# Second exchange of batch 0 through DRAM, products from PSUM, and S1 chunks between the visits

## The chip, the cores and the metric

One core of one Trainium2 chip runs the whole kernel. The metric is the time of one execution on the device, in microseconds (us); the median over runs counts. Engines are named as in the profile: PE is TensorE (PEld its weight loads), DVE VectorE, ACT ScalarE, POOL GpSimd, SP SyncE.

## What is computed

The first half filters each of 8 batches along its 3072 positions in the frequency domain; the second half is a maxout network of two branches over all 24,576 rows.

```python
X = np.fft.rfft(x, axis=1)                       # x: (8, 3072, 256), float32
F = (filt_r + 1j * filt_i)[None, :, :]           # 1537 frequencies x 256 channels
y = np.fft.irfft(X * F, n=x.shape[1], axis=1)
h1, h2 = y.reshape(B * S, D) @ w1, y.reshape(B * S, D) @ w2   # w1, w2: (256, 1024)
out = np.maximum(h1, h2) @ w_out                 # w_out: (1024, 256)
```

## The kernel before, in words

**The transform.** 3072 = 128 x 24, so each transform is done in four steps of matrix products. Step 1 (`f1`) multiplies x by the 128-point table C1 for six chunks of four of the 24 columns; a chunk is called an S1 chunk. The result `at` is written to DRAM (`ad`) and read back in another order as `bt` (`f1_read`): the first exchange. Step 2 (`s2`) applies the 24-point tables U for eight sets of frequencies; a set takes two PSUM banks, `px`. VectorE multiplies px by the filter F into `pq` (`mul`, made of `half` calls). Step 3 (`s3`) multiplies pq by VT into four PSUM banks `pz`, for two sets at a time; these go as `zt` to DRAM (`zd`) and come back as `zr` (`z_read`): the second exchange. s2, mul and s3 for two sets are called a visit; a batch has four. Step 4 (`s4`) multiplies zr by G1 and gives `yt`, 512 rows of y.

**The network.** max(h1, h2) = h2 + relu(h1 - h2). So the kernel keeps Wd = w1 - w2, Wo = w_out and M = w2 @ w_out. `moe_h` computes a block `ph` = Wd^T y and its relu `gt`; `moe_o` sums gt @ Wo and y @ M in `po` and copies it to `ot`, which GpSimd's queue writes out. Column j of block j is taken from Wd with a step of eight columns (L501), since rows p x 8 + c of Wo lie together.

**Order.** All engines run their instructions in the order in which the program emits them. After a prologue for batch 0 comes a loop of 49 tiles of 8 steps; each step has one moe_h, one moe_o of the tile before, and whatever `plan` has put there by hand: s4 at the steps of `z4`, the f1 chunks at `first`, the visits at `visits` or at 48b - 45 + 8v, with the second set's products two steps later and s3 five or six steps later. Which of ScalarE and VectorE copies at, gt and ot is chosen by `pick`, a planner that adds up booked durations; yt and zt are fixed, half each. In the loop, four PSUM banks (`pp`) serve f1, s2, s3 and s4, two serve ph and two po. SyncE issues ad, bt, zd and zr; GpSimd issues x loads, Wo and the output.

**Batch 0** differs. Its step 1 (`f1_0`) writes transposed results into AT, which TensorE transposes into bt (`t1`), so the first exchange stays on the chip. Sets 1, 3, 6 and 7 are copied from PSUM to SBUF by ScalarE (`xs0`), and their products are made from there (`from_xs`): five by GpSimd, three by VectorE; the other sets' products are made from PSUM. Step 3 (`s3_0`) has 128 matmuls of 48 columns a visit and writes the transposed ZT, copied mostly by ScalarE, and `t2` transposes ZT into zr: 8 transposes before the loop, 40 within its steps 0, 2 and 4. Chunk 0 of batch 1 runs before the loop. GpSimd loads batch 1's six x chunks and Wo after its products, and then makes both halves of Wd; x chunks for batch 2 follow as buffers come free.

## Time and profile before

| what | value |
|---|---|
| median of 3 runs | 551.79 us (549.17 to 553.81) |
| the profiled execution | 554.73 us |
| its span, first to last instruction | 553.0 us |
| mean granted TensorE clock | 0.969 |
| first ph of the loop | 63.49 us |
| ph's weight loads | 768, median 144 ns |

The profile shows one execution. A group line gives the line in kernel.py, the engine, the operation, what is written and read, the shape, the count, the busy time, the mean duration in ns, and the idle time of the engine just before with what ended it; a busy TensorE is not one at its peak, since matmuls overlap. Timeline lines give start and length in us, and in brackets the idle time before and its releaser. "issue" is time in which the profile shows nothing that the engine waited for. The clock is the share of the full TensorE clock that was granted.

### The profile page before, as it was taken

Reading aid. Unit: us, or ns where it says so; the run is one execution under the profiler, and the core shown is the slowest. Engines: PE = TensorE matmul, PEld = TensorE weight load, DVE = VectorE, ACT = ScalarE, POOL = GpSimd, SP = SyncE. Lnnn points to the kernel's source line nnn. Section 1 sums busy time; section 2 is a strip of 40 time slices with the busy share of each in tenths; the row PEclk is TensorE's granted clock in tenths of the full one; section 3 lists DMA queues with packets and bytes.
Section 4 is the critical chain, followed back from the end, with each engine's and each line's share of the span. In section 5 each row is a group of like instructions: output and inputs, shape, how many; then the busy total and the mean of one; then the engine's idle time right before and its main releaser. Section 6 shows DMA issues by size and latency. Waiting matters only on the chain.

```text
span 553.0 us, 15465 instructions
## 1 busy us (share of the span) xinstructions
PE 504.2 (91%) x6693; PEld 374.4 (68%) x6693; DVE 329.6 (60%) x541; ACT 348.9 (63%) x609; POOL 76.8 (14%) x127
## 2 busy tenths in 40 slices
PE   3634799998999999998999999999999999999995
PEld 2523567775677767776777777777777777777774
DVE  8397458772587557863867378665776386622220
ACT  8634656575465756675666666676667566666662
POOL 6296001100110011000110011101100000000000
PEclk9975799999899999999999999999999999999998
DMA  7969376768776698579786897769877854421111
GB/s 153 150 193 186 86 146 133 194 174 215 132 163 168 210 210 178 144 227 158 180 185 168 216 186 170 179 213 175 181 172 218 161 148 135 124 106 40 77 77 76
DMA packets 68382, 88.56 MB, mean 160 GB/s; under 512 B 4489, under 2 KB 48674, under 8 KB 67274
## 3 DMA queue, kind: packets, MB, share of 16 engines
q1 hardware_dynamic: 54138, 49.03, 38.2%
q0 software_dynamic: 14176, 38.54, 28.6%
q8 instruction: 52, 0.85, 0.6%
q14 instruction: 16, 0.13, 0.1%
HBM read 53.48 MB, written 47.19 MB: 182 GB/s over the span
## 4 chain that ended last, share of the span: by engine, by line
PE 83%; DMA 9%; issue 2%; ACT 2%; DVE 2%; POOL 1%; SPq 0%; DVEq 0%; POOLq 0%; ACTq 0%
PE ph L501 30%; PE po L524 28%; PE po L519 7%; DMA bt<-ad 6%; PE pz L367 5%; PE py L487 3%; PE pa L310 3%; PE px L331 3%; DMA xb<-in_x_dram 2%; DMA ad<-at 1%; PE pt L410 1%; DVE pq L344 1%; PE pz L456 1%; PE pt L472 1%; POOL xb L109 0%
## 5 line engine op out<-in xcount | busy, mean ns | idle before, releaser
L507 ACT ACTIVATE gt<-ph 128x512 bf16<-128x512 f32 x320 | 191.1, 597 | 117.8 <-PE ph L501 113.1
L501 PE MATMUL ph<-yt,Wd 128*128 128x512 bf16 x768 | 232.7, 385 | 0.6 <-ACT yt L97 0.5
L524 PE MATMUL po<-Wo,gt 128*128 128x256 bf16 x1536 | 230.5, 273 | 0.0
L524 PEld LDWEIGHTS <-gt 128*128 128x128 bf16 x1536 | 150.7, 98 | 49.4 <-issue 0.5
L501 PEld LDWEIGHTS <-Wd 128*128 128x128 bf16 x768 | 94.2, 146 | 23.1 <-issue 12.2
L344 DVE TENSOR_TENSOR pq<-px,Fr 120x512 bf16<-120x512 f32 x120 | 81.2, 680 | 13.1 <-PE px L331 12.1
L535 POOL DMA_DIRECT2D out_dram<-ot x47 | 25.2, 537 | 437.5 <-ACT ot L97 392.5
L344 DVE TENSOR_TENSOR pq<-px,Fi 120x512 bf16<-120x512 f32 x120 | 80.6, 677 | 0.0
L505 DVE TENSOR_SCALAR gt<-ph 128x512 bf16<-128x512 f32 x64 | 43.9, 686 | 53.0 <-PE ph L501 34.8
L519 PE MATMUL po<-M,yt 128*128 128x256 bf16 x384 | 73.5, 273 | 0.0
L99 DVE CAST zt<-pz 112x512 bf16<-112x512 f32 x56 | 36.1, 686 | 52.8 <-PE pz L367 30.5
L101 DVE TENSOR_SCALAR yt<-py 128x512 bf16<-128x512 f32 x48 | 33.2, 691 | 51.4 <-PE py L487 51.4
L519 PEld LDWEIGHTS <-yt 128*128 128x128 bf16 x384 | 37.7, 98 | 36.2 <-issue 0.5
L97 ACT ACTIVATE ot<-po 128x512 f32<-128x512 f32 x81 | 48.4, 598 | 12.9 <-ACT yt L97 7.4
L97 ACT ACTIVATE zt<-pz 112x512 bf16<-112x512 f32 x56 | 30.4, 594 | 27.1 <-PE pz L367 27.1
L99 DVE CAST at<-pa 128x512 bf16<-128x512 f32 x42 | 28.9, 688 | 14.4 <-PE pa L310 14.3
L97 ACT ACTIVATE yt<-py 128x512 bf16<-128x512 f32 x48 | 29.0, 603 | 4.2 <-PE py L487 4.1
L331 PE MATMUL px<-bt,U 48*32 48x256 bf16 x1024 | 22.7, 276 | 9.3 <-DMA bt<-ad 7.4
L367 PE MATMUL pz<-pq,VT 24*64 24x256 bf16 x1792 | 30.4, 271 | 0.0
L97 ACT ACTIVATE at<-pa 128x512 bf16<-128x512 f32 x42 | 25.1, 597 | 8.1 <-PE pa L310 8.0
L487 PE MATMUL py<-G,zr 128*128 128x128 bf16 x384 | 29.4, 219 | 0.2 <-DMA ad<-at 0.2
L109 POOL DMA_DIRECT2D xb<-in_x_dram x48 | 26.2, 556 | 12.6 <-PE py L487 12.6
(111 smaller groups left out, 264.7 us busy)
## 6 DMA issues: line engine op xcount, KB each, us to landing
out_dram<-ot POOLq DMA_DIRECT2D x47, 512.0 KB, 4.1
xb<-in_x_dram POOLq DMA_DIRECT2D x48, 256.0 KB, 6.2
ad<-at SPq DMA_DIRECT2D x42, 256.0 KB
bt<-ad SPq DMA_DIRECT2D x28, 384.0 KB
zd<-zt SPq DMA_DIRECT2D x56, 192.0 KB
zr<-zd SPq DMA_DIRECT2D x28, 384.0 KB
w2f<-in_moe_w_dram SPq DMA_DIRECT2D x1, 1024.0 KB
w1f<-in_moe_w_dram SPq DMA_DIRECT2D x1, 1024.0 KB
```

The costliest lines, as they stand in the source:

```text
L97: S.activation(dst, src, AF.Copy, scale=1.0 if scale is None else scale)
L99: V.tensor_copy(dst, src)
L101: V.tensor_scalar(dst, src, scale, None, OP.mult)
L331: TE.matmul(px[dr][32 * q:32 * q + 32, D * ri:D * ri + D], U[64 * dr:64 * dr + 48, s, ri, q], bt[b][64 * dr:64 * dr + 48, 4 * s + q], star ...
L344: V.tensor_tensor(pq[i][0:120, dr].rearrange("p (r d) -> p r d", r=2), px[dr][0:120].rearrange("p (r d) -> p r d", r=2), F[i][0:120, dr, s ...
L367: TE.matmul(pz[q][64 * dr:64 * dr + 64, D * si:D * si + D], VT[32 * q:32 * q + 24, s, o, 64 * dr:64 * dr + 64], pq[i][32 * q:32 * q + 24, ...
L487: TE.matmul(py[dc][:, 128 * n:128 * n + 128], zr[b][:, 4 * i + n, 128 * dc:128 * dc + 128], G1, start=True, stop=True)
L501: TE.matmul(ph, Wd[:, dc, j::8], y_[:, dc].rearrange("p a b -> p (a b)"), start=(dc == 0), stop=(dc == 1))
L505: V.tensor_scalar(gt[tt][:, j], ph, 0.0, None, OP.max)
L507: S.activation(gt[tt][:, j], ph, AF.Relu)
L519: TE.matmul(p_, y_[:, dc, n], M[:, dc], start=(dc == 0), stop=False)
L524: TE.matmul(p_, g_[:, jj, 128 * n:128 * n + 128], Wo[:, jj], start=False, stop=(jj == 7))
```

## The change

- Batch 0's second exchange goes through DRAM as the other batches' does: s3 takes the place of s3_0, with a choice of copying engines for each visit, z_read is emitted one visit later, and t2, ZT and the plan's t2 steps are gone.
- Set 7 is no longer copied to SBUF: its s2 moves behind the other sets' products, and VectorE makes its products from PSUM, like all of its products now. GpSimd makes the other product of set 6, between the first three and the last three loads of batch 1's x.
- `warm(n)` emits n matmuls of 512 columns into a PSUM bank that nobody reads: 14 during step 1, 3 after each s3 of batch 0, 6 ahead of the loop.
- Wd's columns are stored in block order when it is computed, so that moe_h reads 128 contiguous columns; GpSimd computes one half of Wd, VectorE the other, after batch 0's s3. w2's bf16 copy moves behind them.
- AT moves into the pool of bt, its memset ahead of f1_0; the pq of sets 1 and 3 lie in the setup pool.
- In the loop, batch 1's six chunks run at steps 0 to 5. Batch 2's are put between the visits of batch 1, and those of batch b at 48b - 88, -80, -72, -64, -62 and -61: four of them between the visits of batch b - 1, a step before its s3. f1_read follows two and three steps after. The tables of hand-set steps shrink: batches 2 and 3 get the regular visits, tiles 7 to 17 the regular s4 steps. x loads of batches 3 to 7 are planned five steps earlier. batch 1's last z_read comes a step later.

```diff
--- before.py
+++ after.py
@@ -273,9 +273,9 @@
     def load_wo():
         G.dma_start(out=Wo, in_=moe_w_out.rearrange("(p c) j -> p c j", c=8))
 
-    def prep_wd():
-        for dc in range(2):
-            G.tensor_tensor(Wd[:, dc], w1f[:, dc], w2f[:, dc], OP.subtract)
+    def prep_wd(E, dc):
+        E.tensor_tensor(Wd[:, dc].rearrange("p (c h) -> p c h", c=8), w1f[:, dc].rearrange("p (h c) -> p c h", c=8),
+                        w2f[:, dc].rearrange("p (h c) -> p c h", c=8), OP.subtract)
 
     def prep_w2b():
         for dc in range(2):
@@ -356,7 +356,7 @@
             for i in range(2):
                 half(b, s, i, (dr,))
 
-    def s3(b, v, force=None):
+    def s3(b, v, engines=("act", "dve")):
         pz = banks("pz", 4)
         for si in range(2):
             s = 2 * v + si
@@ -372,7 +372,7 @@
             zd[b] = dram.tile([T, 2, 48, D], BF16, tag="zd", name="zd")
         zt = zpool.tile([128, 2, 4, D], BF16, tag="zt", name="zt")
         for q in range(4):
-            e = ("act", "dve")[q % 2]
+            e = engines[q % len(engines)]
             copy(zt[0:112, :, q], pz[q][0:112].rearrange("p (s d) -> p s d", s=2), 512, force=e)
             book(e, 640)
         for dr in range(2):
@@ -386,9 +386,7 @@
         SP.dma_start(out=zr[b][32 * v:32 * v + 32], in_=src[32 * v:32 * v + 32])
 
 
-    AT = init.tile([128, 2, 2, 64, T], BF16, tag="AT", name="AT")
-    ZT = bpool.tile([128, T, D], BF16, tag="bt", name="ZT")
-    ZV = ZT.rearrange("p t d -> p (t d)")[:, 0:6144].rearrange("p (c t m) -> p c t m", c=2, t=T)
+    AT = bpool.tile([128, 2, 2, 64, T], BF16, tag="bt", name="AT")
 
     def f1_0(c, engines):
         pa = banks("pa")
@@ -418,62 +416,31 @@
         if pool is apool:
             pq_[0, s] = [pool.tile([128, 4, D], BF16, tag="at", name="pq").rearrange("p a d -> p (a d)")
                          .rearrange("p (a c) -> p a c", a=2) for _ in range(2)]
+            return
+        if pool is init:
+            pq = init.tile([128, 2, 2, 512], BF16, tag="pq%d" % s, name="pq")
         else:
-            pq = pool.tile([128, 2, 2, 512], BF16, tag="zt" if pool is zpool else "pq", name="pq")
-            pq_[0, s] = [pq[:, i] for i in range(2)]
+            pq = pool.tile([128, 2, 2, 512], BF16, tag="pq", name="pq")
+        pq_[0, s] = [pq[:, i] for i in range(2)]
 
     xs_ = {}
 
-    def xs0(s, slot, k=0):
-        if slot == "AT":
-            if s == 6:
-                xs_[slot] = init.tile([128, 2, 2, 512], FP32, tag="AT", name="xs")
-            xs_[s] = xs_[slot][:, k]
-        else:
+    def xs0(s, slot):
+        if slot:
             xs = init.tile([128, T, 2, J, 2], FP32, tag=slot, name="xs")
             xs_[s] = xs.rearrange("p t o j h -> p (t o j h)")[:, 0:1024].rearrange("p (a c) -> p a c", a=2)
+        else:
+            xs_[s] = init.tile([128, 2, 512], FP32, tag="xs", name="xs")
         for dr in range(2):
             S.activation(xs_[s][0:120, dr], px_[0, s][dr][0:120], AF.Copy)
 
+    def warm(n):
+        pd, = banks("pd", 1)
+        for i in range(n):
+            TE.matmul(pd, C1, xb[0, 0][:, 0:2].rearrange("p a b -> p (a b)"), start=True, stop=True)
+
     def from_xs(E, s, i):
         product(E, pq_[0, s], xs_[s], i, s)
-
-    pz_ = {}
-
-    def pz0(v):
-        pz_[v] = banks("pz", 4)
-
-    def s3_0(v, engines):
-        pz = pz_[v]
-        for si in range(2):
-            s = 2 * v + si
-            pq = pq_.pop((0, s))
-            for dc in range(2):
-                for dr in range(2):
-                    for n, (o, i, ri) in enumerate(((0, 0, 0), (2, 1, 1), (1, 0, 1), (1, 1, 0))):
-                        for q in range(4):
-                            c = ((dc * 2 + si) * 2 + dr) * 48
-                            TE.matmul(pz[q][:, c:c + 48],
-                                      pq[i][32 * q:32 * q + 24, dr, D * ri + 128 * dc:D * ri + 128 * dc + 128],
-                                      VT[32 * q:32 * q + 24, s, o, 64 * dr:64 * dr + 48], start=(n == 0), stop=(n == 3))
-        for q in range(4):
-            copy(ZV[:, :, 8 * v + q:8 * v + q + 5:4], pz[q][:, 0:384].rearrange("p (c s m) -> p c s m", c=2, s=2), 384,
-                 force=engines[q % len(engines)])
-
-    def t2(n0, n1):
-        if n0 == 0:
-            zr[0] = zrpool.tile([128, N2, D], BF16, tag="zr", name="zr")
-        w = 2 if n0 == 0 else 4
-        for h, n in enumerate(range(n0, n1, w)):
-            pt = bank16("pt")[:, 0:w]
-            for i in range(w):
-                for dc in range(2):
-                    zc = ZV[:, dc].rearrange("p t m -> p (t m)")
-                    TE.transpose(pt[:, i, 128 * dc:128 * dc + 128], zc[:, n + i:n + i + 127 * N2 + 1:N2], I128)
-            if h % 2 == 0:
-                V.tensor_copy(zr[0][:, n:n + w], pt)
-            else:
-                S.activation(zr[0][:, n:n + w], pt, AF.Copy)
 
 
     yt, gt, po, ot = {}, {}, {}, {}
@@ -498,7 +465,7 @@
         y_ = yt[tt]
         ph = psh.tile([128, 512], FP32, tag="ph", name="ph")
         for dc in range(2):
-            TE.matmul(ph, Wd[:, dc, j::8],
+            TE.matmul(ph, Wd[:, dc, 128 * j:128 * j + 128],
                       y_[:, dc].rearrange("p a b -> p (a b)"), start=(dc == 0), stop=(dc == 1))
         pe(430)
         if pick(594, 684) == "dve":
@@ -552,11 +519,13 @@
         load_x(0, c)
     table_c()
     table_u()
+    V.memset(AT[:, :, :, 48:].rearrange("p c a m t -> p (c a) (m t)"), 0.0)
     for c in range(6):
         f1_0(c, ("act", "dve") if c > 4 else ("act", "act"))
         if c < 2:
             fill_f(S, 1, 2048 + 1024 * c, 3072 + 1024 * c)
-    V.memset(AT[:, :, :, 48:].rearrange("p c a m t -> p (c a) (m t)"), 0.0)
+        else:
+            warm(3 if c < 5 else 2)
     load_f(G, 1, (2, 0))
     load_f(SP, 1, (1, 3))
     load_w(SP)
@@ -572,7 +541,7 @@
     t1(2)
     t1(3)
     for s in (1, 3):
-        pq0(s, zpool)
+        pq0(s, init)
     for s in (0, 2, 4, 5):
         pq0(s, pqpool)
     for s in (6, 7):
@@ -582,9 +551,7 @@
     fix_f()
     half(0, 0, 0)
     s2(0, 6)
-    xs0(6, "AT")
-    s2(0, 7)
-    xs0(7, "AT", 1)
+    xs0(6, None)
     table_v()
     s2(0, 4, 5)
     from_xs(G, 1, 0)
@@ -592,27 +559,31 @@
     from_xs(G, 6, 0)
     from_xs(G, 1, 1)
     from_xs(G, 3, 1)
-    for c in range(6):
+    for c in range(3):
         load_x(1, c)
+    from_xs(G, 6, 1)
+    for c in range(3, 6):
+        load_x(1, c)
+    prep_wd(G, 0)
     load_wo()
-    prep_wd()
     half(0, 4, 0)
     half(0, 5, 0)
-    from_xs(V, 7, 0)
     V.memset(F[1][0:1, 0, 0], 0.0)
-    half(0, 0, 1)
-    half(0, 2, 1)
-    half(0, 4, 1)
-    half(0, 5, 1)
-    from_xs(V, 6, 1)
-    from_xs(V, 7, 1)
+    for s in (0, 2, 4, 5):
+        half(0, s, 1)
+    s2(0, 7)
+    half(0, 7, 0)
+    half(0, 7, 1)
     for v in range(4):
-        if v == 2:
-            prep_w2b()
-        pz0(v)
-        s3_0(v, ("act",) if v < 3 else ("act", "dve"))
+        s3(0, v, (("act",), ("act",), ("dve",), ("act", "dve"))[v])
+        if v:
+            z_read(0, v - 1)
+        warm(3)
+    z_read(0, 3)
+    prep_wd(V, 1)
+    prep_w2b()
     prep_w2t()
-    t2(0, 4)
+    warm(6)
     setup.close()
     pp = ctx.enter_context(tc.tile_pool(name="pp", bufs=4, space=bass.MemoryType.PSUM))
     psh = ctx.enter_context(tc.tile_pool(name="psh", bufs=2, space=bass.MemoryType.PSUM))
@@ -620,8 +591,6 @@
     ypool = ctx.enter_context(tc.tile_pool(name="ypool", bufs=4))
     gpool = ctx.enter_context(tc.tile_pool(name="gpool", bufs=2))
     opool = ctx.enter_context(tc.tile_pool(name="opool", bufs=2))
-    for c in range(1):
-        f1(1, c, force=("act", "dve"))
     s4(0)
 
 
@@ -634,24 +603,18 @@
         for c in range(6):
             plan(0, 48 * b + step + every * c, load_x, b, c)
 
-    plan(0, 0, t2, 4, 8)
-    plan(0, 2, t2, 8, 16)
-    plan(0, 4, t2, 16, 24)
     plan(0, 6, prep_m)
-    z4 = {1: 3, 2: 8, 3: 11, 4: 18, 5: 25, 6: 46, 7: 52, 8: 61, 9: 69, 10: 77, 11: 85, 12: 93}
-    z4.update({tt: 8 * tt - 7 for tt in range(13, 18)})
+    z4 = {1: 3, 2: 8, 3: 11, 4: 18, 5: 25, 6: 46}
     for tt in range(1, 6 * B):
         plan(0, z4.get(tt, 8 * tt - (5 if tt % 6 == 0 else 6)), s4, tt)
-    first = {1: (0, 1, 2, 3, 4), 2: (39, 40, 41, 42, 43, 44), 3: (86, 87, 88, 89, 90, 91), 4: range(131, 137)}
-    visits = {1: (12, 19, 26, 33), 2: (54, 62, 70, 78), 3: (100, 108, 116, 124)}
+    first = {1: range(6), 2: (16, 23, 30, 37, 39, 40)}
+    visits = {1: (12, 19, 26, 33)}
     for b in range(1, B):
         if b > 1:
-            plan_x(b, -94, 5)
-        ns = first.get(b, range(48 * b - 62, 48 * b - 56))
-        for c, n in zip(range(6 - len(ns), 6), ns):
+            plan_x(b, -94 if b == 2 else -99, 5)
+        n = 48 * b
+        for c, n in enumerate(first.get(b, (n - 88, n - 80, n - 72, n - 64, n - 62, n - 61))):
             plan(0, n, f1, b, c)
-        plan(0, n + 2, f1_read, b, 0)
-        plan(0, n + 3, f1_read, b, 1)
         for v in range(4):
             n = visits[b][v] if b in visits else 48 * b - 45 + 8 * v
             plan(0, n, s2, b, 2 * v, 2 * v + 1)
@@ -661,7 +624,11 @@
             if v:
                 plan(0, n, z_read, b, v - 1)
             plan(0, n, s3, b, v)
-        plan(0, n + (4 if b > 1 else 3), z_read, b, 3)
+        plan(0, n + 4, z_read, b, 3)
+    for b in range(1, B):
+        n = {1: 5, 2: 40}.get(b, 48 * b - 61)
+        plan(0, n + 2, f1_read, b, 0)
+        plan(0, n + 3, f1_read, b, 1)
 
     clock.update(pe=0.0, act=0.0, dve=0.0)
     for tt in range(6 * B + 1):
```

## The prediction, made before the changed kernel was run

> **What bounds the kernel now.** I read the page first (engine shares, slices, chain), then the busy time by stage, then TensorE's timeline at the places where a stage has holes, then the waits, SyncE's timeline, and Wd's tile.
>
> The page:
> ```profile
> PE 504.2 (91%) x6693; PEld 374.4 (68%) x6693; DVE 329.6 (60%) x541; ACT 348.9 (63%) x609; POOL 76.8 (14%) x127
> PE   3634799998999999998999999999999999999995
> PEclk9975799999899999999999999999999999999998
> PE 83%; DMA 9%; issue 2%; ACT 2%; DVE 2%; POOL 1%; SPq 0%; DVEq 0%; POOLq 0%; ACTq 0%
> ...
> L524 PEld LDWEIGHTS <-gt 128*128 128x128 bf16 x1536 | 150.7, 98 | 49.4 <-issue 0.5
> ```
> TensorE is the bound from the fifth slice on; the other engines have a third of their time free. So there are three places to win: the first 63 us, where TensorE is mostly idle; the few holes later (the 9% DMA); and the spacing of the products themselves.
>
> Busy time by stage (PE, PEld, DVE, ACT, POOL, granted clock, DMA share, GB/s):
> ```profile
> 40.00:44.00 4.00, 2.33 (x158) 1.89 (x161) 4.00 (x8) 1.19 (x4) 4.00 (x8) 0.50 0.44 56
> 44.00:48.00 4.00, 0.89 (x89) 0.76 (x79) 4.00 (x1) 0.45 (x2) 4.00 (x3) 0.50 1.11 203
> 52.00:56.00 4.00, 1.50 (x128) 1.37 (x128) 0.00 (x0) 1.60 (x5) 0.00 (x0) 0.50 1.00 192
> 136.00:139.00 3.00, 0.00 (x0) 0.00 (x0) 0.00 (x0) 0.00 (x0) 0.00 (x0) 1.00 1.22 175
> 141.00:142.00 1.00, 1.00 (x6) 0.74 (x5) 1.00 (x2) 0.58 (x1) 0.00 (x0) 0.50 0.71 84
> ```
> Between 40 and 58 us batch 0's second step runs at half the clock with TensorE mostly idle; from 52 to 56 VectorE is idle too, so no engine is the bound there. At 136 us all engines stand still, and afterwards the clock is 0.50 until about 143.
>
> TensorE's timeline, and the longest waits:
> ```profile
> 43.74 1.10 PE L456 MATMUL pz<-VT,pq 24*128 24x48 bf16 x91 [0.38 <-DVE pq L344]
> 47.96 1.50 PE L456 MATMUL pz<-VT,pq 24*128 24x48 bf16 x128 [3.11 <-issue]
> 53.88 1.50 PE L456 MATMUL pz<-VT,pq 24*128 24x48 bf16 x128 [4.42 <-issue]
> 57.88 0.54 PE L456 MATMUL pz<-VT,pq 24*128 24x48 bf16 x34 [2.50 <-issue]
> 63.49 0.85 PE L501 MATMUL ph<-yt,Wd 128*128 128x512 bf16 x2 [0.51 <-ACT yt L97]
> ```
> ```profile
> PE pz L456 <- issue: 10.0, 3, 4.4
> PE px L331 <- DMA bt<-ad: 7.4, 4, 3.5
> ```
> Three idle stretches, 10.0 us together, end on nothing that the profile shows, each after 128 matmuls and as many weight loads. The first product of the main loop, ph, comes at 63.49. Later TensorE waits four times for bt, the read-back of step 1: 1.28 us in batch 1 (until 82.02), 3.51 in batch 2 (until 139.36), 2.6 in batches 3 and 4 together.
>
> SyncE's timeline of batch 1's exchange, and Wd's tile:
> ```profile
> 99.53 0.93 SPq L379 DMA_DIRECT2D zd<-zt  x2
> 105.04 0.31 SPq L386 DMA_DIRECT2D zr<-zd  x1
> 108.74 0.88 SPq L379 DMA_DIRECT2D zd<-zt  x2
> 112.33 0.31 SPq L386 DMA_DIRECT2D zr<-zd  x1
> ```
> ```profile
> L501 PEld LDWEIGHTS <-Wd x768: 141/144/171, 62.8 to 541.0; 128*128 128x128 bf16 x192
> ```
> A quarter (one of four visits) is written in 5.5 us (99.53 to 105.04) with x loads in flight, in 3.6 without. Loading Wd takes 144 ns where gt's weights take 98 (the last line of the page's above).
>
> **The change, part by part.**
>
> Up to the products. The memset of AT (0.91 us, behind the last AT copy) moves into the 2.59 us that VectorE idles before that copy, so the transposes may begin 1.1 us earlier than 19.18. Little of it reaches the end: GpSimd's first product starts at 28.14 after 11.10 us of waiting for a filter DMA, VectorE's at 28.32. I count 0.2. The unread products after the first chunks are 14 of 216 ns in holes of up to 1.9 us between x chunks: nothing; without the holes they would cost 3 us. The dropped copy of set 7 frees ScalarE 1.0 us before VT and two PSUM banks for which table_v waited 0.67: VectorE reaches its last Fr products about 0.7 us sooner, 35.5 instead of 36.2.
>
> The products. VectorE loses three products from SBUF (2.35, and 7.79 for two) and takes four from PSUM at 0.62 apart (8 in 4.87), 2.5. Its end goes from 51.4 to 35.5 + 0.25 (memset) + 4.87 + 2.5 = 43.1. GpSimd takes one more: five at 2.33 (6.98 for three) from 28.1 end at 39.8, three x loads at 0.55 make 41.4, the sixth product ends at 43.8; then three loads (45.4), half of Wd (2.41, with the strided read up to twice that), Wo at 47.8.
>
> The second step. 128 matmuls of 48 columns a visit become 64 of 256, which took 1.01 us at full clock (batch 1), 2.0 at half. Visit 0 can begin when set 4's banks are free, 39.4; visit 1 needs set 7's banks, 43.1; with the unread triples (1.3 at half clock) visit 3 would end at 49.3. Evacuation: four copies on one engine 2.0 to 2.5 us, on two 1.25. zt has two buffers, so visit 2's copies wait for write 0 and visit 3's for write 1, and each read waits on SyncE for its write, with the next write queued behind it. GpSimd's seven x loads and Wo keep DMA busy until about 55 (now eight and Wo, issued from 40.66 to 49.6, until 57), so I price a write at 5.1 us from its second issue while they run, 3.3 after, and a read at 5.3 (121.28 to py at 126.75) or 3.3. Write 0: 43.6 to 48.9. Write 1: 47.2 to 52.5. Visit 2's copies 48.9 to 51.4, its write lands at 56. Visit 3's copies 52.5 to 53.8, written by 57.2, read by 60.6. Then py, yt and ph take 1.4, as now: ph at 62.0, against 63.49, **-1.5**. Bounds: all DMAs at their uncontended price, ph at 58.9; all writes held until the loads are through at 55, ph at 67.5. I take the middle because the loads come in two groups. ScalarE's w2b (2.02), w2b's transposes, VectorE's half of Wd (1.2 by the 1.76 of 1536 elements, at most 4.8 like GpSimd's) and the six unread products fall between 53.8 and 60.6; they cost up to 2 us if that cover goes.
>
> The 5.5 against 3.6 us are the row for who goes first. The Trainium skill (DMA: Bandwidth & Descriptors, Queues, rings and completion order) says that each DMA engine takes turns between queues, packet by packet; writes would then hardly wait for loads, the sum would be 3.1 lower (rival 4), and the row speaks against it.
>
> The loop until batch 1's visits. t2's 40 transposes (2.24 us at 56 ns) and their copies go; f1 of chunk 0 comes in (0.43). Steps 0 to 5 now take 9.3 us from ph to the last write of ad (63.49 to 72.83); then six f1, six gt and one yt pair, 20 copies of 0.6 to 0.69 on two engines, 7.1. Write and read of ad follow as now (72.83 to 82.02, 9.2): 16.3 instead of 18.5. Against it I put 0.7 for a cold clock: TensorE has idled, and after the stall at 136 it ran at 0.50 for 3 us. **-1.5** (0 to -2.2). The 1.28 us wait for bt stays.
>
> S1 chunks. For batch 2 the last f1 moves from step 44 to 40 and the first px from 54 to 51: 11 steps of 0.98 and two s4 of 0.44, 11.7 us, for a chain of 14 now (125.4 to 139.36) in which six writes of ad crowd a z read, and one out and one x load get between the two halves of the read. With the chunks spread and both of those issued behind the first half I expect about 12: 3.5 falls to 0.5, **-3.0** (-1.5 to -3.5). A stall that short leaves the clock up: 3.2 us at half clock were 1.6 lost, **-1.5**. Batches 3 and 4 get 16 steps between last f1 and px instead of 9 and 11: **-2.6**. Against this, f1 now stands one step (0.98) before s3 in 24 visits, and both draw on four banks. In a visit now VectorE's products end at 326.56 and s3 starts at 327.06; f1 pushes s3 to 327.49, and pa's copies, one on each engine by the planner's own arithmetic in most visits, end near 327.0 and 327.25. That fits by 0.2 us; I price it at +0.5 in all (0 to 1.0 a visit, +24). The z read of batch 1 comes one step later, +0.4.
>
> Wd. After s2 and s3 (56 places) ph's pair takes 0.49 to the next product (328.07 to 328.56) instead of 0.43; elsewhere the load is hidden behind a matmul of 216 ns. With contiguous columns I expect the 0.06 to go: **-3.0** (0 to -4).
>
> Sum: -1.5 -1.5 -3.0 -1.5 -2.6 -3.0 +0.9 = -12.2. The profiled execution took 554.7 (span 553.0 and 1.7 around it), so 542.5; it lies 2.9 above the median of the three runs, so **539.6** as a median.
>
> **Rivals.**
> 1. The exchange is late: writes wait for the loads to drain, ph at 67.5 and 0.8 more of cold clock. +6.3, 545.9. For it: 5.5 us under loads; against: they come in two groups.
> 2. The other side: s3 waits for f1's banks. If one of pa's copies gets two VectorE operations ahead of it (1.2, less the 0.2 of slack), s3 starts 1.0 late in 24 visits: +24 in place of the 0.5, 563. It decides from 0.3 us a visit (the gain falls below 1%), and from 0.76 the kernel is slower by 1%. For it: so little slack; against: six f1 in consecutive steps now run through the same banks with no hole.
> 3. The "issue" gaps belong to the visit, not to the number of instructions. I take them for the fetch of code: queue 8 of the page moves 52 packets of 16 KB, one for 257 of TensorE's 13,386 instructions; a visit now has 256, and the DMA view shows four such packets from 45 to 60. Half as many instructions meet a fetch half as often. If each visit pays 3.1 as now, visit 3 ends at 39.4 + 3 x (2.0 + 1.3 + 3.1) + 2.0 = 60.6 and ph comes near 70.6; with 0.8 of cold clock 549. The gaps, each after one such block, speak against it. The Trainium skill (Runtime: NRT & Kernel Launch, Instruction fetch mechanics) holds the fetch mostly hidden, which speaks for it.
> 4. Writes do not wait for the loads: ph at 58.9, 536.5. Against it: the 5.5 us above.
>
> **How the numbers follow.** The forecast 0.54, rival 1 0.18, rival 2 0.13, rival 3 0.07, rival 4 0.05, others 0.03 (0.01 faster, 0.02 slower). A measurement here can tell about 1%, 5.5 us: below 546.3 is faster. Rival 1 lies on that bound, 0.08 faster and 0.10 not. Faster 0.54 + 0.08 + 0.05 + 0.01 = 0.68, within 1% 0.10 + 0.07 = 0.17, slower 0.13 + 0.02 = 0.15. The forecast's own range is 532.5 (entry at 58.9, Wd -4, the rest at its better end) to 546. The range wanted reaches over rivals 1 and 3 to 554; rival 2 is left out.
>
> **What would show it.** ph's first start near 62 (58.9 to 67.5), at most one "issue" hole over 2 us in batch 0's visits; px waiting for bt at most 0.5 us in batch 2 and not in batches 3 and 4; no 0.50 clock after 100 us; Wd's load at 98 ns and ph after s2 and s3 in 0.43; PE without waits before pz in the visits. A ph later than 68, or waits of pz for pa's copies, would prove me wrong.

## The result, and the profile after

The changed kernel took 557.47 us (median of 16 runs, 553.15 to 560.05) against 553.34 for the kernel before beside it (16 runs, 548.42 to 557.92): ratio 1.0095, 95% interval 1.0067 to 1.0123. It is slower by about 1%; the forecast was 539.6. The profiled execution took 558.43 us (span 556.7), 3.7 more in span than the one of before.

The page of the changed kernel (engine totals; TensorE's busy tenths and granted clock in 40 slices; the chain of waits; Wd's weight loads):
```profile
PE 511.9 (92%) x6418; PEld 347.2 (62%) x6418; DVE 320.9 (58%) x539; ACT 345.6 (62%) x604; POOL 77.4 (14%) x127
...
PE   3757397997999999999999999999999999999995
...
PEclk9876588999899999999999999999999999999998
...
PE 84%; DMA 8%; ACT 2%; DVE 2%; issue 1%; POOL 1%; SPq 0%; DVEq 0%; POOLq 0%; ACTq 0%
...
L468 PEld LDWEIGHTS <-Wd 128*128 128x128 bf16 x768 | 69.3, 98 | 28.7 <-issue 13.3
```
Three things changed as meant: TensorE runs fewer matmuls (6418 recorded for 6693), Wd's load takes 98 ns, and "issue" fell from 2% to 1% of the chain. But the DMA's 8% has hardly moved from 9%: waits for transfers went in one place and came in another. The digit 3 in the fifth slice (55.7 to 69.6 us) stands where before had 7.

TensorE's timeline, at the two places that decide:
```profile
69.62 0.61 PE L454 MATMUL py<-G,zr 128*128 128x128 bf16 x8 [1.90 <-DMA zr<-zd]
70.82 0.84 PE L468 MATMUL ph<-yt,Wd 128*128 128x512 bf16 x2 [0.59 <-ACT yt L97]
...
140.37 1.01 PE L454 MATMUL py<-G,zr 128*128 128x128 bf16 x8 [4.16 <-DMA zr<-zd]
```
The main loop's first ph starts at 70.82 instead of 63.49. And at 140.37 TensorE has waited 4.16 us for the last read of batch 1's second exchange: a wait that before did not have. In the waits of the whole run:
```profile
PE py L454 <- DMA zr<-zd: 6.1, 2, 4.2
...
PE px L331 <- DMA bt<-ad: 3.0, 2, 2.3
```
The waits of px for bt, 7.4 us in four places before, are 3.0 in two, both in batch 1. Those of batches 2, 3 and 4 are gone, and so are the three "issue" holes before pz.

SyncE's timeline, in batch 0's exchange and before the wait at 140:
```profile
44.35 4.43 SPq L379 DMA_DIRECT2D zd<-zt  x4
51.33 0.32 SPq L386 DMA_DIRECT2D zr<-zd  x1
54.01 1.22 SPq L379 DMA_DIRECT2D zd<-zt  x2
60.26 0.31 SPq L386 DMA_DIRECT2D zr<-zd  x1
...
128.87 0.82 SPq L379 DMA_DIRECT2D zd<-zt  x2
130.05 1.69 SPq L313 DMA_DIRECT2D ad<-at  x2
132.79 0.33 SPq L386 DMA_DIRECT2D zr<-zd  x1
```
A read is issued when its write has landed. Visit 0's write, issued from 44.35, is read at 51.33; visit 1's, issued by 48.78, only at 60.26, some 12 us later. Since zt has two buffers, VectorE's copies of visit 2 waited for the first write (7.46 us, until 51.50) and the copies of visit 3 for the second (ScalarE 12.39 us, until 60.31). The DMA view of the first write's stretch, 44.35 to 51.40 us, gives for each queue its packets, MB and the time that its packets took as a share of 16 engines:
```profile
q0 software_dynamic: 586, 1.07, 88.4%
q1 hardware_dynamic: 801, 0.39, 19.3%
```
GpSimd's queue (q0: x, later Wo) takes nearly all of the time of the engines, and SyncE's (q1) gets 0.39 MB through, in 801 packets to the other's 586.

Busy time by stage (columns as before):
```profile
52.00:62.00 10.00, 1.81 (x61) 1.00 (x60) 3.65 (x7) 1.69 (x3) 0.27 (x1) 0.61 1.10 249
...
71.00:74.00 3.00, 3.00 (x8) 1.01 (x7) 1.42 (x3) 1.37 (x3) 0.53 (x1) 0.55 0.05 9
91.00:94.00 3.00, 3.00 (x15) 1.73 (x14) 2.97 (x6) 1.20 (x2) 0.00 (x0) 0.63 1.03 131
...
140.00:143.00 3.00, 2.63 (x15) 1.84 (x16) 0.69 (x1) 1.19 (x2) 0.00 (x0) 0.50 1.02 180
```
From 52 to 62 every engine has time and the DMA share is 1.10: the DMA engines are the bound there. The clock is low three more times behind waits: 0.55 as the loop begins, 0.63 after px's wait until 90.23, 0.50 after the wait at 140.

Where the time lies, by the end of the same gt in both profiles (changed minus before, us): at the loop's first gt +7.3; at step 13, behind batch 1's waits for bt, +8.2; at step 46 +9.7; at step 47, behind the wait at 140, +14.4; at step 56, behind before's own stall, +9.7; at the last +3.7.

### The profile page after: what moved, and what is told of

Read it like the earlier page. It is cut to its first block, busy times and chain, and to the rows that moved or that the text cites. A ratio compares the mean times of both kernels' runs of the same rounds, so it can differ in the third digit from the quotient of the medians.

```text
span 556.7 us, 14943 instructions
## 1 busy us (share of the span) xinstructions
PE 511.9 (92%) x6418; PEld 347.2 (62%) x6418; DVE 320.9 (58%) x539; ACT 345.6 (62%) x604; POOL 77.4 (14%) x127
## 4 chain that ended last, share of the span: by engine, by line
PE 84%; DMA 8%; ACT 2%; DVE 2%; issue 1%; POOL 1%; SPq 0%; DVEq 0%; POOLq 0%; ACTq 0%
PE ph L468 30%; PE po L491 29%; PE po L486 7%; PE pz L367 6%; PE py L454 4%; DMA zd<-zt 3%; PE pa L310 3%; PE px L331 3%; DMA xb<-in_x_dram 2%; DMA zr<-zd 1%; DMA bt<-ad 1%; DVE pq L344 1%; ACT zt L97 1%; ACT xs L435 1%; PE pt L408 1%
## 5 line engine op out<-in xcount | busy, mean ns | idle before, releaser
L474 ACT ACTIVATE gt<-ph 128x512 bf16<-128x512 f32 x314 | 187.5, 597 | 114.1 <-PE ph L468 112.6
L468 PEld LDWEIGHTS <-Wd 128*128 128x128 bf16 x768 | 69.3, 98 | 28.7 <-issue 13.3
L472 DVE TENSOR_SCALAR gt<-ph 128x512 bf16<-128x512 f32 x70 | 48.0, 686 | 66.8 <-ACT gt L474 34.7
L99 DVE CAST zt<-pz 112x512 bf16<-112x512 f32 x62 | 39.9, 686 | 53.2 <-PE pz L367 32.8
L97 ACT ACTIVATE zt<-pz 112x512 bf16<-112x512 f32 x66 | 35.6, 595 | 49.9 <-PE pz L367 36.2
L97 ACT ACTIVATE ot<-po 128x512 f32<-128x512 f32 x82 | 49.0, 597 | 15.9 <-ACT yt L97 9.3
L367 PE MATMUL pz<-pq,VT 24*64 24x256 bf16 x2048 | 39.6, 285 | 1.8 <-DVE zt L99 1.2
L367 PEld LDWEIGHTS <-VT 24*64 24x64 bf16 x2048 | 28.6, 110 | 12.5 <-issue 7.0
L454 PE MATMUL py<-G,zr 128*128 128x128 bf16 x384 | 29.7, 221 | 6.1 <-DMA zr<-zd 6.1
L97 ACT ACTIVATE at<-pa 128x512 bf16<-128x512 f32 x51 | 29.4, 596 | 3.7 <-PE pa L310 1.6
L454 PEld LDWEIGHTS <-zr 128*128 128x128 bf16 x384 | 25.7, 99 | 8.4 <-issue 7.2
```

The source lines that it names most:

```text
L97: S.activation(dst, src, AF.Copy, scale=1.0 if scale is None else scale)
L99: V.tensor_copy(dst, src)
L367: TE.matmul(pz[q][64 * dr:64 * dr + 64, D * si:D * si + D], VT[32 * q:32 * q + 24, s, o, 64 * dr:64 * dr + 64], pq[i][32 * q:32 * q + 24, ...
L454: TE.matmul(py[dc][:, 128 * n:128 * n + 128], zr[b][:, 4 * i + n, 128 * dc:128 * dc + 128], G1, start=True, stop=True)
L468: TE.matmul(ph, Wd[:, dc, 128 * j:128 * j + 128], y_[:, dc].rearrange("p a b -> p (a b)"), start=(dc == 0), stop=(dc == 1))
L472: V.tensor_scalar(gt[tt][:, j], ph, 0.0, None, OP.max)
```

## The experiments

Each is the changed kernel with the edit shown, unless another base is named. Ratios are to the kernel before, beside it on the same chip. Kernels are compared by their ratios, since the medians of before went from 553.3 to 555.9. e2, e3 and e7 rest on four runs each, e9 on six, the others on eight or more. Single executions differ from the start (GpSimd's first product begins between 26.4 and 30.3 us), so the table also gives the time from there to the first py.

| kernel | median us | ratio (95%) | first ph | product to py |
|---|---|---|---|---|
| before | 553.34 | 1 | 63.49 | 34.2 |
| changed | 557.47 | 1.0095 (1.0067 to 1.0123) | 70.82 | 39.5 |
| e1_no_loads | 550.38 | 0.9944 (0.9902 to 0.9986) | 61.65 | 33.1 |
| e2_zt3 | 559.90 | 1.0156 (1.0111 to 1.0201) | 68.61 | 40.9 |
| e6_loads_early | 554.45 | 0.9973 (0.9932 to 1.0013) | 67.10 | 36.2 |
| e12_wo_late | 555.17 | 1.0015 (0.9971 to 1.0060) | 66.80 | 38.0 |
| e8_no_warm | 557.49 | 1.0036 (1.0000 to 1.0072) | 70.96 | 41.9 |
| e5_onchip | 548.33 | 0.9890 (0.9852 to 0.9929) | 61.32 | 29.5 |
| e11_best | 548.11 | 0.9898 (0.9859 to 0.9937) | 61.26 | 31.5 |
| e3_plan_before | 557.79 | 1.0118 (1.0044 to 1.0191) | 67.40 | 38.4 |
| e7_onchip_cover | 548.03 | 0.9865 (0.9806 to 0.9925) | 59.07 | 29.5 |
| e10_x_after_out | 556.06 | 1.0049 (1.0014 to 1.0083) | 69.44 | 40.2 |
| e9_cover_x | 543.73 | 0.9833 (0.9778 to 0.9888) | 59.12 | 29.7 |
| e4_wd_only (on before) | 552.45 | 0.9953 (0.9916 to 0.9991) | 64.40 | 35.8 |

The changed prologue, untouched in the changed kernel, e3 and e10, takes 38.4 to 40.2 in the last column: differences of that size between single profiles say nothing.

### Why the main loop starts late

**No x loads beside the exchange.**
```diff
+    load_wo()
+    for c in range(2): load_x(2, c)
+    for c in range(6): xb[1, c] = xb[0, c]
     from_xs(G, 1, 1)
     from_xs(G, 3, 1)
-    for c in range(3): load_x(1, c)
     from_xs(G, 6, 1)
-    for c in range(3, 6): load_x(1, c)
     prep_wd(G, 0)
-    load_wo()
...
-        for c in range(6):
+        for c in range(2 if b == 2 else 0, 6):
```


> The changed kernel, but batch 1's six x loads are left out (its step 1 uses batch 0's chunks, so part of the computation is changed), and Wo and two x chunks of batch 2 are loaded ahead of GpSimd's third product; no GpSimd load is then under way when batch 0's second exchange runs. Theory A (the exchange's transfers are held behind GpSimd's loads): each write lands 3 to 4 us after its issue instead of 6.9 and 12, the first ph comes at 59 to 62 instead of 70.8, and the time falls by 8 to 11 us. Theory B (the exchange is slow by itself: two zt buffers, write after copy after write): ph at 67 or later, gain under 3 us.

The second write was read at 50.08 instead of 60.26, and py came 5.3 to 7.1 us sooner after GpSimd's first product. SyncE's timeline of e1:
```profile
41.64 4.42 SPq L379 DMA_DIRECT2D zd<-zt  x4
46.18 0.89 SPq L386 DMA_DIRECT2D zr<-zd  x1
49.15 0.82 SPq L379 DMA_DIRECT2D zd<-zt  x2
50.08 0.95 SPq L386 DMA_DIRECT2D zr<-zd  x1
```
The loads are what holds the exchange, and the ratio is 1.5% below the changed kernel's. This kernel leaves out six loads and is no faster version, only a test. With them, no order of the transfers tried here reached its ph at 61.65. Yet even alone the exchange takes 18.6 us from its first write to py (41.64 to 60.25).

**A third buffer for zt.**
```diff
-    zpool = ctx.enter_context(tc.tile_pool(name="zpool", bufs=2))
+    zpool = ctx.enter_context(tc.tile_pool(name="zpool", bufs=3))
```


> The changed kernel with three zt buffers instead of two: visit 2's copies no longer wait for write 0, visit 3's wait for write 0 and not write 1, so write 3 is issued near 54.5 instead of 61.7. Theory A (held behind the loads until about 61): writes 2 and 3 still land near 61 to 62, ph comes 3 to 4 us earlier, near 67, time 3 to 4 us less. Theory B (the buffers make the chain): write 3 lands near 58.3, ph near 63, time 7 us less.

Visit 2's copies and s3 no longer wait, and neither theory's gain comes: TensorE only waits longer at the end.
```profile
67.22 1.01 PE L454 MATMUL py<-G,zr 128*128 128x128 bf16 x8 [11.09 <-DMA zr<-zd]
```
The buffers are not the limit; the transfers are.

**The loads ahead of the exchange.** GpSimd issues the six loads and Wo behind its third product, from 36.6 to 40.3.
```diff
     from_xs(G, 1, 0)
     from_xs(G, 3, 0)
-    from_xs(G, 6, 0)
     from_xs(G, 1, 1)
+    for c in range(6): load_x(1, c)
+    load_wo()
     from_xs(G, 3, 1)
-    for c in range(3): load_x(1, c)
+    from_xs(G, 6, 0)
     from_xs(G, 6, 1)
-    for c in range(3, 6): load_x(1, c)
     prep_wd(G, 0)
-    load_wo()
```


> The changed kernel with all six x loads of batch 1 and Wo issued between GpSimd's third and fourth product (near 37 to 41 us, where DMA is nearly idle) and nothing left out. Theory A (the loads hold the writes of the second exchange): the loads are through near 51, writes 2 and 3 and all reads run free, ph at 62 to 65, 6 to 8 us less than the changed kernel. Theory B (not the loads but the products feeding step 3, which now come later from GpSimd): ph stays at 69 or later.

The first write (from 43.77) still landed only by 51.89, but the second by 55.50. The entry gained 2.2 to 4.0 us, less than theory A expected (ph at 67.10, not 62 to 65), while the ratio fell by 1.2%, 6.7 us, as it expected.

**Wo and batch 2's first loads behind the exchange.** This is to tell apart whether the order of issue holds the writes or the sum of what the DMA engines have to do.
```diff
-    def z_read(b, v):
+    def z_read(b, v, E=SP):
-        SP.dma_start(out=zr[b][32 * v:32 * v + 32], in_=src[32 * v:32 * v + 32])
+        E.dma_start(out=zr[b][32 * v:32 * v + 32], in_=src[32 * v:32 * v + 32])
...
     prep_wd(G, 0)
-    load_wo()
...
-    z_read(0, 3)
+    z_read(0, 3, G)
+    load_wo()
```


> The changed kernel, but GpSimd issues Wo's load, and so also the loads of x(2,0) and x(2,1), only behind the last read of batch 0's exchange, which it issues in SyncE's place; nothing else moves. In the changed kernel's trace, from 41.69 to 69.62 (27.93 us), GpSimd's queue moved 2.40 MB and took 50.3% of the 16 DMA engines, 14.0 us, and SyncE's took 43.4%, 12.1 us: 26.1 us of work in 27.9. Theory D: the exchange is late because this sum of DMA time fills the stretch, whoever was issued first. About 0.8 MB of the loads (Wo and x(2,0)) leave it, 4.8 us by the 14.0 for 2.40 MB; the second read is issued near 55.5 instead of 60.26, py starts at 65 instead of 69.6 (63.5 to 66.5), and the ratio to the kernel before falls from 1.0095 to 1.001 (0.996 to 1.005). Theory H: a write waits only for the loads that were issued before it. Wo (51.16) and x(2,0) (51.73) were issued after the second write (by 48.78), so the second read is still issued at 59 or later, py comes at 68 or later, and the ratio stays at 1.006 or more.

SyncE's timeline of e12:
```profile
41.74 5.19 SPq L379 DMA_DIRECT2D zd<-zt  x4
...
54.41 0.89 SPq L386 DMA_DIRECT2D zr<-zd  x1
```
The second read comes 12.7 us after the first write (41.74 to 54.41). With the unchanged prologue it came 15.9 after in the changed kernel (44.35 to 60.26), 14.3 in e3 (42.22 to 56.47) and 16.7 in e10 (41.84 to 58.57). So loads issued later than a write seem to hold it too, against theory H, by 1.6 us at the least, but this is one profile beside three that differ by 2.4. The ratio, 1.0015, is theory D's, and its interval ends just below the changed kernel's. But py moved by only 0.4 to 2.2 us after GpSimd's first product, not by 4.8: at the end the last write landed at 61.1 and its read took until 65.38, with the moved loads beside it. The account that fits is that the DMA's total time is the bound while loads and writes overlap, and after that the chain of one write and one read.

**Batch 0's exchange on the chip again.** s3_0, ZT and t2 come back; the products, Wd and the loop's tables stay as changed, and the unread products remain in step 1 alone.
```diff
-        s3(0, v, (("act",), ("act",), ("dve",), ("act", "dve"))[v])
-        if v:
-            z_read(0, v - 1)
-        warm(3)
-    z_read(0, 3)
+        if v == 2: prep_w2b()
+        pz0(v)
+        s3_0(v, ("act",) if v < 3 else ("act", "dve"))
...
-    prep_w2b()
-    warm(6)
+    t2(0, 4)
...
+    plan(0, 0, t2, 4, 8)
+    plan(0, 2, t2, 8, 16)
+    plan(0, 4, t2, 16, 24)
```


> The changed kernel with batch 0's second exchange on the chip again (s3_0, ZT and t2 as before, no unread products after step 1); products from PSUM, GpSimd's split loads, Wd and the S1 chunks stay as changed. Theory A (the exchange through DRAM is what makes the entry late): the first ph comes at 60 to 64, within 2 us of the 63.5 of the kernel before, and the time falls by 5 to 8 us below the changed kernel's, below the kernel before's. Theory B (the products, the moved loads or Wd make the entry late): ph stays beyond 67.

Product to py fell to 29.5: 9 to 11 us below the changed prologue, and 4.7 below before's. The ratio fell by 2.0% from the changed kernel's. So the way through DRAM costs the 4.7 us that the rest of the new prologue gains, and as much again. How much of the 4.7 is due to the products from PSUM was not tested by itself: TensorE also has only two "issue" holes here, 7.3 us together, where before has three, 10.0.

**Without the unread products.**
```diff
-        else:
-            warm(3 if c < 5 else 2)
...
-        warm(3)
...
-    warm(6)
```


> The changed kernel without its unread products. Theory A (they do not reach the end: step 1's lie in holes, those between the visits run while the exchange is waited for, and the last six end before the clock matters): ph within 1.5 us of the changed kernel's, its first steps at half clock either way, time the same within 2 us. Theory B (they keep the clock up): visits and first loop steps slower, time 3 us more. Theory C (they cost): the visits end 3 to 4 us earlier and ph comes earlier by as much.

The median is that of the changed kernel within 0.02 us, while the ratios' intervals just touch. No gain from them shows; whether they cost up to 0.6% is open. In its one profile e8 has an "issue" hole of 2.71 us before pz, which the changed kernel's does not have, and its py comes 1.7 us later than the latest of the changed prologue's.

**The "issue" holes without loads beside them.** e9 (below) with e6's order of loads.

> The kernel before this one in the list, with all six loads of batch 1 and Wo issued between GpSimd's third and fourth product. Theory A (a fetch of code also queues behind GpSimd's loads, so the issue holes of 3.4 to 4.2 us in the on-chip step 3 shrink to about 2.5 when no load is under way): ph at 57 to 59, 1 to 3 us less. Theory B (the holes are the fetch's own length): the holes stay, ph at 59 to 61.

TensorE's timeline of e11:
```profile
46.22 1.50 PE L467 MATMUL pz<-VT,pq 24*128 24x48 bf16 x128 [3.42 <-issue]
51.04 1.50 PE L467 MATMUL pz<-VT,pq 24*128 24x48 bf16 x128 [3.32 <-issue]
55.59 0.66 PE L467 MATMUL pz<-VT,pq 24*128 24x48 bf16 x45 [3.05 <-issue]
```
and its busy time in the second of these holes:
```profile
47.70:51.00 3.30, 0.02 (x2) 0.00 (x0) 0.00 (x0) 2.70 (x5) 3.30 (x2) 0.50 0.35 71
```
With the DMA at 0.35 the hole is as long as with it at 1.15 (the first), so the loads do not make it; each comes with a 16 KB packet of queue 8. The expectation of a better version was a miss: in the last column its entry is 1.9 us later than e9's, which has two such holes, 7.5 us together, where e11 has three, 9.8. Between steps 98 and 104 it lost another 4.2 us to e9, with px waiting up to 3.5 us for bt. Which transfer was late there is open.

### Why batch 1's last tile waits

**The tables of before**, with batch 1's six chunks still at steps 0 to 5.
```diff
-    z4 = {1: 3, 2: 8, 3: 11, 4: 18, 5: 25, 6: 46}
+    z4 = {1: 3, 2: 8, 3: 11, 4: 18, 5: 25, 6: 46, 7: 52, 8: 61, 9: 69, 10: 77, 11: 85, 12: 93}
+    z4.update({tt: 8 * tt - 7 for tt in range(13, 18)})
-    first = {1: range(6), 2: (16, 23, 30, 37, 39, 40)}
-    visits = {1: (12, 19, 26, 33)}
+    first = {1: range(6), 2: (39, 40, 41, 42, 43, 44), 3: (86, 87, 88, 89, 90, 91), 4: range(131, 137)}
+    visits = {1: (12, 19, 26, 33), 2: (54, 62, 70, 78), 3: (100, 108, 116, 124)}
...
-            plan_x(b, -94 if b == 2 else -99, 5)
+            plan_x(b, -94, 5)
```


> The changed kernel with the loop's hand-set steps of the kernel before (S1 chunks bunched again, its visits and s4 steps; batch 1's six chunks stay at steps 0 to 5). Theory A (the stall for bt in batch 2 only moved to the read of zr, because the chunks had covered it): the wait of py for zr in tile 6 falls from 4.2 us to under 1, the wait of px for bt in batch 2 returns to about 3.5, those of batches 3 and 4 to about 2.6 together; the time is 2 to 3 us more than the changed kernel's. Theory B (the late zr read is a consequence of the prologue, whatever the steps): the 4.2 us stay, and the time is 6 us more.

```profile
PE px L331 <- DMA bt<-ad: 7.0, 6, 2.2
```
The wait for zr at tile 6 is gone, and px waits 7.0 us for bt in six places: 2.8 in batch 1, 3.9 in batches 3 and 4, but only 0.2 in batch 2, where theory A expected 3.5. So with the chunks bunched again the stall of batch 2 did not come back, in the one execution profiled (554.34 us, the fastest of four): its bt was there 7.2 us after the first issue (134.40 to 141.55), not 10.3 as in before (129.03 to 139.36), and the x load issued behind it landed only after 12.0 us instead of 7.1. The ratio cannot be told from the changed kernel's, with an interval of some 4 us either way. In the profiles the spread chunks and earlier x loads take away 4.1 us of waits in batches 2 to 4 and bring one of 4.16.

**Two chunks back as cover**: on e5, batch 2's chunks of steps 30 and 37 go behind batch 1's last s3, to steps 39 to 42 with the last two, and batch 2's visits come three steps later (batch 3's chunks likewise, tiles 7 to 12 as before, and batch 1's last z_read a step earlier again).
```diff
-    first = {1: range(6), 2: (16, 23, 30, 37, 39, 40)}
-    visits = {1: (12, 19, 26, 33)}
+    first = {1: range(6), 2: (16, 23, 39, 40, 41, 42), 3: (59, 67, 75, 83, 85, 86)}
+    visits = {1: (12, 19, 26, 33), 2: (54, 62, 70, 78)}
```


> The changed kernel with the on-chip exchange of batch 0 as in the experiment before, and with four of batch 2's S1 chunks put back behind the last s3 of batch 1 (steps 39 to 42; batch 2's visits three steps later, batch 3's chunks five steps behind each s2). Theory A (the chunks had covered the wait for zr in tile 6): py's wait of 3.7 us in tile 6 falls to about 1, px's wait for bt in batch 2 stays under 1.5, no half clock follows, and the time is 3 to 4 us below that of the on-chip kernel with the changed steps. Theory B (total chain: what is won at py is lost at px): no change within 1 us.

```profile
128.03 1.03 PE L498 MATMUL py<-G,zr 128*128 128x128 bf16 x8 [3.22 <-DMA zr<-zd]
```
A miss: these two chunks alone, 0.87 us of work, leave 3.22 us of the 3.74 in e5. An x load of batch 3 was issued at 118.28, between that write of zd (116.64) and its read (120.63), as it is in the changed kernel at 130.50 (write 128.87, read 132.79).

**That load later**: the changed kernel, batch 3's loads from step 48 on instead of 45.
```diff
-            plan_x(b, -94 if b == 2 else -99, 5)
+            plan_x(b, {2: -94, 3: -96}.get(b, -99), 5)
```


> The changed kernel with one number changed: batch 3's x loads are planned from step 48 on instead of 45, so that GpSimd issues the first of them behind the output of tile 4 and not right behind that of tile 3, between the last write of zd and the read of zr. Theory A (loads issued ahead of a transfer hold it up): the read of zr lands about 2 us sooner, py's wait in tile 6 falls from 4.2 to near 2, and with a stall that short no half clock follows (1.2 us more): 2 to 3.5 us less from tile 6 on. Theory B (only the four chunks that moved away had covered it): the wait stays at 4 us.

```profile
137.79 0.61 PE L454 MATMUL py<-G,zr 128*128 128x128 bf16 x8 [1.56 <-DMA zr<-zd]
```
4.16 falls to 1.56, though f1 then waits 2.2 us once for an x chunk, and the ratio falls by 0.5%, with intervals that overlap.

**Both**, on the chip: e7 with e10's edit.

> The on-chip kernel with four chunks behind the last s3 of batch 1, whose wait had stayed at 3.2 us, with the x loads of batch 3 from step 48 on as well. Theory A: both together take py's wait in tile 6 to under 1 us, and the time falls by 3 us more, to near 545 or a ratio of 0.981. Theory B (the chain is as long whatever is ahead of it): wait and time stay.

The waits of e9:
```profile
PE px L331 <- DMA bt<-ad: 4.0, 3, 2.1
...
PE py L498 <- DMA zr<-zd: 1.1, 1, 1.1
```
At 0.9833 (0.9778 to 0.9888) it beats before by 1.7%, and it is the best version here: products from PSUM, Wd in block order, the exchange of batch 0 on the chip, the chunks spread with cover behind them, batch 3's loads behind the read. Its interval overlaps e7's, so the last edit by itself is shown by the wait, not by the time.

### Wd alone

The kernel before with only Wd's columns in block order, GpSimd still making both halves.
```diff
-            G.tensor_tensor(Wd[:, dc], w1f[:, dc], w2f[:, dc], OP.subtract)
+            G.tensor_tensor(Wd[:, dc].rearrange("p (c h) -> p c h", c=8), w1f[:, dc].rearrange("p (h c) -> p c h", c=8),
+                            w2f[:, dc].rearrange("p (h c) -> p c h", c=8), OP.subtract)
...
-            TE.matmul(ph, Wd[:, dc, j::8],
+            TE.matmul(ph, Wd[:, dc, 128 * j:128 * j + 128],
```


> The kernel before with nothing changed but Wd stored in block order (GpSimd still computes both halves, now from strided reads). Theory A (the strided load costs ph 50 ns at each place behind s2 or s3, 56 places and a few behind py): Wd's load at 98 ns, ph's pair 50 ns shorter there, 3 us less, ratio 0.9945. Theory B (the load is hidden anyway, or GpSimd's strided work delays the entry by as much): ratio 0.998 to 1.002.

0.9953 is 2.6 us (0.5 to 4.6) of gain; the three "issue" holes, 11.2 us, and px's four waits for bt, 7.1, stay as they were.

## Why the prediction was wrong

The spans differ by +3.7 us where the sum said -12.2. By the ends of gt:

| part | predicted | profile |
|---|---|---|
| first ph | -1.5 | +7.3 |
| to batch 1's first visit | -1.5 | +0.9 |
| to step 46 | 0 | +1.5 |
| steps 46 to 56 (batch 2's stall, its clock, the z read) | -4.1 | +0.1 |
| the rest: batches 3 and 4, Wd, s3's banks | -5.1 | -6.0 |

Wd's term and that of s3's banks run over the whole loop and stand whole in the last row.

**The step that failed is "ph at 62.0, -1.5".** The products were right: VectorE's end at 44.0 (priced 43.1; 51.4 before). Then each write was priced by itself, at 5.1 us from its second issue, while "they come in two groups". From their second issues (44.75 and 48.30) the first two took 6.6 and 12.0 us; with the same prologue it was 6.0 and 10.3 in e3, 10.1 and 12.8 in e10. What the step left out is the sum of the work. The trace of before had the loads' part; from 40 to 58 us:
```profile
q0 software_dynamic: 1296, 2.62, 81.2%
```
These are loads of x and Wo, 14.6 us of all 16 engines. The exchange's own part is in e1, from the first write to py (18.61 us):
```profile
q1 hardware_dynamic: 3392, 3.15, 69.2%
```
That is 12.9 us. In the changed kernel both pass between the first load (41.69) and py, and its DMA view from 41.69 to 69.62 shows how they fill the stretch:
```profile
q0 software_dynamic: 1170, 2.40, 50.3%
q1 hardware_dynamic: 3392, 3.15, 43.4%
```
50.3% and 43.4% of 27.93 us are 26.2. The shares are no strict bound, since they can add up to more than 100% (108% in the stretch from 44.35); but the DMA share was 1.08 from 44.35 to 51.40, 1.13 from there to 60.26 and 0.82 after it, so the engines were full until about 60. The price of 3.3 us for a transfer after the loads was low as well: in e1, without any load, the last write took 4.4 us from its second issue and its read 4.1 (51.73, 56.17, 60.25), and the whole chain 18.6 us where the forecast had 17.0 with loads beside it (43.6 to 60.6).

That is rival 1, the late exchange, whose mechanism the runs bear out (e1, e6), but with a bound that was too low: its 67.5 assumed that the loads are through at 55. They were not through before about 60. Wo was issued at 51.16 where the forecast had 47.8: the products began 2.0 us later in this execution, and GpSimd's half of Wd took 3.88 us instead of 2.41. What the exchange took from the loads in turn is not separated. The same prologue gave ph at 67.4, 69.4 and 70.8 in three profiles (e3, e10 and the changed kernel), so up to 3.4 us of the 7.3 belong to this execution.

On rival 4, the Trainium skill (DMA: Bandwidth & Descriptors, Queues, rings and completion order) says that a DMA engine takes turns between queues packet by packet. The trace does not speak against the page: from 44.35 to 51.40 there were 586 packets of loads and 801 of writes, though no view shows when both queues had packets waiting. The forecast read "writes would then hardly wait" from it, and took the 5.5 us row to speak against it; the reading was wrong. A load's packet took 170 ns (88.4% of 16 x 7.05 us, by 586) and a write's 27 (19.3%, by 801), so if the engines take turns packet by packet, the queue with the long packets has them most of the time.

**"-1.5" until batch 1's visits** came out +0.9. TensorE had idled 8.34 us until 62.40, and the loop began at 0.55 of the clock, for which 0.7 was booked; and batch 1's wait for bt, said to stay at 1.28, became 3.0, with 0.63 of the clock behind it, most likely the 1.5 us lost up to step 46.

**"+0.4" for batch 1's z read** was mis-sized tenfold: 4.16 us and half the clock after it. The stall of batch 2, -3.0, and its clock, -1.5, are gone as forecast, though e3 leaves open whether spreading the chunks did it; and a stall as long came eight steps earlier, at step 46. Two edits made it: the four chunks moved ahead had been 1.7 us of cover (4 x 0.43) between s3 and s4 of tile 6, and the x loads planned five steps earlier put one between the write and its read, which then took 7.6 us to py (132.79 to 140.37) instead of 5.5 (121.28 to 126.75). Undoing both, with the rest of the tables, takes the wait away (e3). The load alone leaves 1.56 (e10); on the chip, half of the cover alone leaves 3.22 (e7), the load and half of the cover 1.1 (e9). The forecast counted steps for bt and looked at nothing else that those chunks had hidden.

**Right:** -2.6 in batches 3 and 4 (px waits there no longer, and 3.9 us come back in e3); Wd's -3.0:
```profile
L468 PEld LDWEIGHTS <-Wd x768: 95/98/152, 70.0 to 544.7; 128*128 128x128 bf16 x192
```
with 0.44 us from ph to the next product after s3 (333.55 to 333.99) instead of 0.49, and 0.47% in e4; and rival 2 fell: s3 is not pushed out by f1, and the only waits of pz for VectorE's products, 0.5 us in three, lie in the prologue. Of the loop's last part, 0.9 us of gain has no step. One sum does not come out: the lower end of the forecast's own range, 532.5, is 533.8 by the better ends that are given; nothing rests on it.

**Rival 3** fell too: with half as many matmuls the visits lost their holes, as the forecast had it (one of 2.71 us is left in e8, without the unread products); of 128 + 128 instructions a visit again (e5, e9, e11) they return at 3.05 to 3.87 us each. That they are the fetch of code is inferred from the 16 KB packet beside each. The Trainium skill (Runtime: NRT & Kernel Launch, Instruction fetch mechanics) calls the fetch mostly hidden; if the holes are the fetch, the trace disagrees for these short matmuls. But removing 10.0 us of holes was worth less than the exchange through DRAM cost.

## What to carry to other kernels

Before transfers are put on a path that sets the end, add up the DMA time of everything that is under way in that stretch, from the queues' shares, and compare the sum with the stretch: a single transfer's latency under load is no price when the loads fill the engines. And when work is moved out of a place, list every wait that it covered there, and every load that its new order puts between a write and its read; here one stall went and another as long came at the other exchange.

## What the hardware showed that was not expected

- After 256 instructions that run in 1.5 us, TensorE stands for 3.05 to 3.42 us (e11), each time with one 16 KB packet of queue 8, most likely the next block of code. In e11 this is so with the DMA at a share of 0.35 as with 1.15. Before's holes were 3.11, 4.42 and 2.50 us, with the DMA at 1.11, 1.09 and 0.22; why they differ more is open.
- GpSimd's subtraction of 1024 columns with a step of 8 floats took 3.88 us where before's contiguous one took 2.41; VectorE's took 2.03 with the step.
- A transfer issued later seems to hold one issued earlier on another queue: without Wo and x(2,0), both issued after it, the second write was read 1.6 to 4.1 us sooner after the first (e12, one profile beside three).
